# A planned scan-and-mixture kernel: one-chunk units at the start, ten late gate products on VectorE, six late copies on ScalarE, new ranks

## The chip, the cores and the metric

The kernel runs on one core of a Trainium2 chip. The metric is the device time of one execution in microseconds, the median over runs. A profile of a single execution gives a trace of every instruction on the engines: TensorE (PE, with its weight loads as PEld), VectorE (DVE), ScalarE (ACT), GpSimd (POOL), and SyncE (SP), which here only issues transfers.

## The reference

The input is a sequence `a`, `b` of 8 x 6400 rows of 128 numbers. A first-order recurrence runs along each sequence, and its output goes through a mixture of eight low-rank adapters, of which each row uses two.

```
h = a[:, t] * h + b[:, t];  out[:, t] = h          # scan, per batch, 6400 steps
x = out.reshape(51200, 128)
logits = x @ w_gate                                # 8 experts
topk = two largest;  w = softmax over the two
delta = sum over the two of w * ((x @ A[e]) @ B[e])    # rank 16
return x + delta
```

## The kernel before, in words

The 51,200 rows are cut into 100 chunks of 512 rows, each of four blocks of 128 rows. Rows arrive with time along the partitions, so each chunk is first turned.

The front of chunk c: `la`/`lb` load 256 KB of each input (two chunks in one transfer of 512 KB, except for the first `HEAD` chunks, which come singly); PE turns a into `pA` and b into `pB` (L562; for chunks loaded as a pair `P{c}` turns b of chunk c and a of chunk c+1 together, by half-height pieces); ACT copies `pA` to `a_st` (`ae`, L580); DVE runs the recurrence into `xT` (`sc`, L613), which continues from the last column of the chunk before.

A unit is a run of blocks, six before the tail, four in the last four units. `Z{u}` (L633) multiplies its blocks by A and the gate weights together into `pZ`, and ACT copies that to `zl` (`ze`, L639). Units are taken together in gate groups (four units, 24 blocks, six chunks, then smaller ones by `TAPER`). `gating` works out both largest logits and the weights for the whole group: maxima on DVE (`g1`, `g4`), the wide elementwise steps on POOL (`q2` to `q7`, L669 to L680) or, for the last six groups (`WIDE_DVE`), on DVE, a sigmoid on ACT (`w1`, L682), and the weights `g` on DVE (`g8`, L688).

The back of chunk c: the gate product `zw = zl * g` on POOL (`mu`, L707) or on DVE (`md`, L711); PE turns it (`T`, L720); the turned product is copied from PSUM to `zwT` by DVE (`te`, L729) or by ACT (L726); PE adds x itself (L734) and the product with B (L735) in `D`; ACT copies the sum to `outt` (`oe`, L744); SP stores two chunks at a time (`st`, L779), the last four singly.

The PSUM banks for T and D are two, used in turn (`place`): T of chunk c waits for `oe` of chunk c-2. For the last twelve chunks (`TAIL_CHUNKS`), once no more chunk has to be turned, the four banks of `pA` and `pB` join them. There are four `zw` buffers, six pair buffers for each input, 24 chunks of `xT` and 18 chunks of `outt`.

The order of the work is planned when the program is built. Every operation gets a rank: a base by its chunk, plus `TEMPLATE` by its kind, plus `NUDGE` by its name. `schedule` takes the operations engine by engine, the one that can begin first among those whose rank lies within `WINDOW` of the lowest, by its own assumed durations and rates (`LOAD_RATE`, `STORE_RATE`, `PAIR_RATE` and the like). The result is a fixed order on each of the five engines, and on SP the order of all transfers. At run time each engine goes through its list in order, and waits by semaphores only. Thus an operation that waits holds up whatever stands behind it on its engine.

These settings decide what the change touches: `HEAD` (chunks loaded singly), `LEAD` (sizes of the first gate groups, empty before), `TE_LAST` and `MU_DVE` (chunks counted from the end: 1 is chunk 99), `SPLIT` (stores that are cut into two transfers by partitions), `te_act`, `un`, and the list of units.

Of the kernel before, what the change touches and what calls it, by code (L numbers as in the profile page):

```python
# [10 lines left out]
PERIOD = 6  # L11
# [8 lines left out]
LOAD_RATE = 392e3  # L20
STORE_RATE = 408e3
# [86 lines left out]
START = (-999, "", 0)  # L108
FIRST = -9999
EARLY = -400  # L110
LEAD = []
TAPER = [2, 2, 1, 1, 1, 1]
WIDE_DVE = [1, 2, 3, 4, 5, 6]
TE_LAST = []
TAIL_UNITS = [4, 4, 4, 4]
TE_ACT = [1]
MU_DVE = [1, 2, 4, 6, 8]
TAIL_CHUNKS = 12
WARM0 = 12
WARM = 16  # L120
HALVES = 0.745
# [758 lines left out]
```

## Time and profile before

| what | value |
|---|---|
| median of 3 runs | 207.53 us (207.46 to 207.57) |
| the profiled execution's own time | 207.91 us |
| its span, first to last instruction | 205.9 us |
| its mean granted TensorE clock | 0.975 |
| moved by transfers | 79.26 MB, mean 385 GB/s |

Spans and starts in the rows below are counted from the first instruction of the profiled execution. In a row of a timeline stand the start, the duration, the engine, the line, the operation, the tiles (output, then inputs), the count, and in brackets how long the engine had been idle before and what released it. A row of the chain of waits has a start, a duration, an engine, a tile and a line. A row of the table by stretches has the busy time and the number of instructions of PE, PEld, DVE, ACT and POOL, then the granted TensorE clock, the DMA share and GB/s.

### The profile page before, as it was taken

The numbers are of one execution on the slowest core, as the hardware profiler recorded it, in microseconds if no ns is written. First come the engines' busy times: TensorE is split into PE (matmuls) and PEld (weight loads), VectorE is DVE, ScalarE is ACT, GpSimd is POOL, SyncE is SP. The second block draws the span as 40 slices with busy tenths as digits, with TensorE's granted clock in tenths as the row PEclk, the third lists the DMA queues.
The fourth block names the chain that finished last, engine by engine and source line by source line (L and its number), as shares of the span: only waits on it lengthen the run. The fifth ranks groups of instructions, "written<-read, shape, count | busy, mean of one in ns | idle before, by whom it ended". The sixth has DMA issues, their size and how long they took to land.

```text
span 205.9 us, 7539 instructions
## 1 busy us (share of the span) xinstructions
PE 184.7 (90%) x3152; PEld 160.9 (78%) x3152; DVE 177.7 (86%) x289; ACT 169.1 (82%) x306; POOL 144.6 (70%) x176
## 2 busy tenths in 40 slices
PE   7779589999998899899799999999999999879683
PEld 6557478887897789788689888988888888857572
DVE  0789688998998899798899999999997999989881
ACT  2356668999998999899799999999999998886372
POOL 1000328879898978878788988899989898687420
PEclk9999958999999999999999999999999999999789
DMA  6999999999999999999999999999999999997388
GB/s 191 368 392 415 405 409 406 405 409 405 411 417 406 414 403 417 409 403 416 408 409 400 409 395 408 415 410 411 409 412 410 410 409 404 405 352 289 132 299 300
DMA packets 30559, 79.26 MB, mean 385 GB/s; under 512 B 3774, under 2 KB 3902, under 8 KB 30526
## 3 DMA queue, kind: packets, MB, share of 16 engines
q1 hardware_dynamic: 29054, 78.39, 97.1%
q10 hardware_dynamic: 1472, 0.40, 0.8%
q8 instruction: 25, 0.41, 0.8%
q14 instruction: 8, 0.07, 0.1%
HBM read 52.56 MB, written 26.21 MB: 383 GB/s over the span
## 4 chain that ended last, share of the span: by engine, by line
PE 67%; DVE 12%; DMA 10%; POOL 3%; issue 3%; SPq 2%; ACT 1%; DVEq 0%; POOLq 0%
PE pA L562 14%; PE pB L562 12%; PE pZ L633 11%; PE pO L734 10%; PE pO L720 10%; PE pO L735 9%; DMA a_tm<-in_a_dram 7%; DVE xT L613 5%; DMA b_tm<-in_b_dram 3%; POOL zw L707 3%; SPq L541 2%; DVE zwT L729 2%; DVE zw L711 1%; ACT outt L744 1%; DVE g L688 1%
## 5 line engine op out<-in xcount | busy, mean ns | idle before, releaser
L613 DVE TENSOR_TENSOR_SCAN xT<-a_st,xT,pB 128x512 f16<-128x512 f32 x96 | 120.3, 1253 | 9.5 <-PE pA L562 5.6
L707 POOL TENSOR_TENSOR zw<-zl,g 128x512 f16<-128x512 f32 x95 | 100.4, 1069 | 24.7 <-PE pO L720 11.3
L562 PE MATMUL pB<-ident_f,b_tm 64*128 64x64 f32 (+1 forms) x768 | 71.4, 235 | 6.5 <-DMA a_tm<-in_a_dram 2.8
L580 ACT COPY a_st<-pA 128x512 f32<-128x512 f32 x100 | 60.5, 612 | 17.5 <-PE pA L562 16.0
L562 PE MATMUL pA<-ident_f,a_tm 64*128 64x64 f32 (+1 forms) x768 | 71.7, 235 | 2.0 <-DMA a_tm<-in_a_dram 1.0
L562 PEld LDWEIGHTS pB<-ident_f,b_tm 64*128 64x128 f32 (+1 forms) x768 | 57.9, 142 | 12.5 <-issue 3.7
L562 PEld LDWEIGHTS pA<-ident_f,a_tm 64*128 64x128 f32 (+1 forms) x768 | 57.9, 142 | 8.2 <-DMA a_tm<-in_a_dram 2.3
L639 ACT COPY zl<-pZ 128x816 f32<-128x816 f32 (+1 forms) x68 | 58.0, 853 | 2.3 <-PE pZ L633 1.6
L744 ACT COPY outt<-pO 128x512 f32<-128x512 f32 x92 | 52.7, 609 | 7.7 <-PE pO L735 7.3
L734 PE MATMUL pO<-ident_h,xT 128*128 128x128 f16 x368 | 50.1, 223 | 1.2 <-DVE zwT L729 1.0
L735 PE MATMUL pO<-cst_h,zwT 128*128 128x128 f16 x368 | 48.9, 220 | 0.8 <-issue 0.8
L734 PEld LDWEIGHTS pO<-ident_h,xT 128*128 128x128 f16 x368 | 40.5, 114 | 4.8 <-DVE zwT L729 2.1
L633 PE MATMUL pZ<-cst_h,xT 128*128 128x136 f16 x400 | 36.5, 228 | 1.5 <-DVE xT L613 0.6
L735 PEld LDWEIGHTS pO<-cst_h,zwT 128*128 128x128 f16 x368 | 36.9, 100 | 0.8 <-issue 0.8
L720 PE MATMUL pO<-ident_h,zw 128*128 128x128 f16 x368 | 33.2, 221 | 2.0 <-ACT outt L744 1.3
L729 DVE COPY zwT<-pO 128x512 f16<-128x512 f16 x77 | 30.2, 410 | 3.4 <-PE pO L720 3.1
L633 PEld LDWEIGHTS pZ<-cst_h,xT 128*128 128x128 f16 x400 | 27.1, 115 | 4.4 <-DVE xT L613 1.3
L720 PEld LDWEIGHTS pO<-ident_h,zw 128*128 128x128 f16 x368 | 22.3, 98 | 6.0 <-issue 1.9
L669 POOL TENSOR_TENSOR k<-zl,m 128x192 f32<-128x192 f32 x15 | 7.8, 519 | 22.9 <-DVE m L667 22.9
L671 POOL TENSOR_SCALAR L<-k 128x192 f32<-128x192 f32 x15 | 12.9, 860 | 1.3
L613 DVE TENSOR_TENSOR_SCAN xT<-a_st,pB 128x512 f16<-128x512 f32 (+1 forms) x8 | 7.5, 939 | 4.6 <-PE pB L562 4.3
L678 POOL TENSOR_TENSOR L<-k,m 128x192 f32<-128x192 f32 x15 | 7.9, 524 | 2.8 <-DVE m L676 2.7
(41 smaller groups left out, 106.1 us busy)
## 6 DMA issues: line engine op xcount, KB each, us to landing
a_tm<-in_a_dram SPq DMA_DIRECT2D x46, 512.0 KB, 10.7
b_tm<-in_b_dram SPq DMA_DIRECT2D x46, 512.0 KB, 10.6
out_dram<-outt SPq DMA_DIRECT2D x46, 512.0 KB, 10.8
a_tm<-in_a_dram SPq DMA_DIRECT2D x8, 256.0 KB, 5.8
b_tm<-in_b_dram SPq DMA_DIRECT2D x7, 256.0 KB, 6.0
out_dram<-outt SPq DMA_DIRECT2D x4, 256.0 KB, 2.7
out_dram<-outt SPq DMA_DIRECT2D x2, 480.0 KB
b_tm<-in_b_dram ACTq DMA_DIRECT2D x1, 256.0 KB, 3.6
```

Of the source, the lines that this page charges most:

```text
L562: last = eng["pe"].transpose(*args)
L580: lambda: eng["act"].copy(a_st[c % NA][:, :], pA[:, c % 2, :]), fr(c, "ae"))
L613: last = eng["dve"].tensor_tensor_scan(out=x[:, s0:s1], data0=a_st[c % NA][:, s0:s1], data1=pB[:, c % 2, s0:s1], initial=init, op0=ALU.mul ...
L633: last = eng["pe"].matmul(pZ[:, k // (n // 2), o : o + W], xblock(b0 + k), Awg_h)
L639: return eng["act"].copy(zl[:, zb : zb + n, :].rearrange("p (h k) w -> p h (k w)", h=2), pZ[:, :, 0 : n // 2 * W])
L671: lambda e: e.tensor_scalar(out=ll, in0=kk, scalar1=0.0, scalar2=-1.0e30, op0=ALU.is_ge, op1=ALU.mult), dve=not main)
L707: lambda: eng["pool"].tensor_tensor(out=wv, in0=zv, in1=gv, op=ALU.mult), ba(gi, c, "mu"))
L720: last = eng["pe"].transpose(ptile[:, k * 128 : k * 128 + 128], zw[w][:, k, :], ident_h[:, :])
L729: lambda: eng["dve"].tensor_copy(zwT[w][:, :], ptile[:, 0:C]), ba(gi, c, "te"))
L734: eng["pe"].matmul(dst, xblock(b0 + k), ident_h[:, :], start=True, stop=False)
L735: last = eng["pe"].matmul(dst, zwT[w][:, k * 128 : k * 128 + 128], B_h, start=False, stop=True)
L744: lambda: eng["act"].copy(outt[:, o0 : o0 + n, :].rearrange("p k w -> p (k w)"), bank),
```

## The change

The first 24 blocks are now six units of four blocks (one chunk each) and no longer four units of six; `LEAD` makes gate groups of one, two and three of them. Behind that the groups again cover six chunks each, on the same boundaries (chunks 6, 12, 18 and so on), and the last six groups cover the same chunks as before. Only the first four chunks are loaded singly; chunks 4 to 7 now come in pairs. The gate products of chunks 90 to 99 are all on DVE (before: 92, 94, 96, 98 and 99). The copies to `zwT` of chunks 90, 92, 94, 96, 98 and 99 go from DVE to ACT. The stores of chunks 56 and 78 were each cut into 120 and 8 partitions; now only that of chunk 56 is cut, into 125 and 3. All ranks and the windows are new, and three of the assumed rates.

```diff
-LOAD_RATE = 392e3
-STORE_RATE = 408e3
+LOAD_RATE = 387e3
+STORE_RATE = 413e3
...
-WINDOW = {'pe': 16.262, 'act': 17.153, 'dve': 47.02, 'pool': 47.064, 'sp': 57.831}
+WINDOW = {'pe': 32.272, 'act': 25.764, 'dve': 40.575, 'pool': 41.697, 'sp': 31.952}
...
-LEAD = []
+LEAD = [1, 2, 3]
...
-TE_LAST = []
+TE_LAST = [1, 2, 4, 6, 8, 10]
 TAIL_UNITS = [4, 4, 4, 4]
+HEAD_UNITS = [4, 4, 4, 4, 4, 4]
 TE_ACT = [1]
-MU_DVE = [1, 2, 4, 6, 8]
+MU_DVE = [1, 2, 3, 4, 5, 6, 7, 8, 9, 10]
...
-PAIR_RATE = 411e3
-HEAD = 8
+PAIR_RATE = 414.5e3
+HEAD = 4
...
-SPLIT = {56: [120, 8], 78: [120, 8]}
+SPLIT = {56: [125, 3]}
...
-    for n in [U] * ((NBLK - sum(TAIL_UNITS)) // U) + TAIL_UNITS:
+    for n in HEAD_UNITS + [U] * ((NBLK - sum(HEAD_UNITS) - sum(TAIL_UNITS)) // U) + TAIL_UNITS:
...
         def un(u, kind):
-            return (PERIOD * (u // GMAX), kind, u % GMAX)
+            v = u - len(HEAD_UNITS)
+            if v < 0:
+                return ((units[u][0] + units[u][1] - 1) // J - 1, kind, 0)
+            return (sum(HEAD_UNITS) // J + PERIOD * (v // GMAX), kind, v % GMAX)
```

What the planner makes of it, in the names used above (lists of the instruction order, no times in them):

```
PE, from chunk 96's turn on
before  P96 Z63 D77 T78 P97 T79 D78 Z64 P98 B99 Z65 T80 D79 D80 T81 T82 D81 ...
after   P96 T79 D78 D79 P97 T80 Z65 P98 T81 B99 D80 D81 Z66 T82 T83 D82 ...
D finished on PE ahead of P30, P60, P97:  before 10, 39, 78;  after 14, 39, 80
DVE, the end
before  sc97 g8(84-89) g2 g3 g5 ... te84 sc98 ... sc99 te86 ... te88 ... md94 ... md92 g8 te89 ... md96 ... md99 md98 te99 te98
after   g8(84-89) ... sc97 ... te80 te81 sc98 ... te82 sc99 te83 te84 ... te86 md90 ... te87 ... md91 ... te88 ... md92 ... te91 te89 md93 ...
        ... md96 ... te93 ... md97 ... md95 ... te97 ... md94 ... te95 ... md99 ... md98
POOL, the last gate products
before  ... mu89 mu90 mu91 mu95 mu93 mu97
after   ... mu87 mu88 mu89
SP, the first stores and the last loads
before  la30 lb30 st0 la32 lb32 la34 st2 lb34 ...     ... st58 la98 lb98 st60 st62 st64 ...
after   la30 lb30 la32 st6 lb32 la34 lb34 la36 st0 st8 st2 lb36 ...     ... st58 lb96 st60 la98 lb98 st62 st64 ...
```

More of the change, by code (lines that the diff above doesn't have):

```diff
@@ L121 @@
 HALVES = 0.745
-PAIR_RATE = 411e3
-HEAD = 8
+PAIR_RATE = 414.5e3
+HEAD = 4
 TAIL = 0
 STORE_TAIL = [1, 1, 1, 1]
-SPLIT = {56: [120, 8], 78: [120, 8]}
+SPLIT = {56: [125, 3]}
 TEMPLATE = {
-    "la": [-13.284, -13.376, -10.147],
-    "lb": [-12.856, -11.393, -13.112],
-    "A": [3.619, 4.619, -4.264, 6.619, 7.619, 8.619],
-    "B": [-2.245, 2.718, -8.407, 8.99, 6.061, 4.41],
-    "ae": [-1.493, 12.357, 10.831, 7.96, 5.931, 11.772],
-    "sc": [-2.149, -1.286, 6.521, -19.69, -9.638, -0.216],
-    "Z": [6.623, 2.916, -2.696, 9.959],
-    "ze": [6.413, 12.686, 18.636, 4.611],
-    "g1": [1.078],
-    "g2": [15.192],
-    "g3": [12.311],
-    "g4": [-7.624],
-    "g5": [43.586],
-    "g6": [18.91],
-    "w1": [27.261],
+    "la": [-13.694, -9.66, -7.958],
+    "lb": [-12.181, -8.232, -7.954],
+    "A": [0.032, 1.032, 2.032, 3.032, 98.725, 5.032],
+    "B": [-11.554, -16.992, -3.625, -1.674, -6.236, -9.416],
+    "ae": [-17.948, -9.336, -10.605, 9.499, -11.379, -1.476],
+    "sc": [-6.402, -11.561, 14.237, 14.579, 0.092, 8.857],
+    "Z": [15.334, 15.322, 3.164, 15.937],
+    "ze": [11.98, 9.742, 7.383, 9.214],
+    "g1": [12.595],
+    "g2": [-8.826],
+    "g3": [10.93],
+    "g4": [7.91],
+    "g5": [-34.789],
+    "g6": [-12.133],
+    "w1": [11.331],
     "w2": [27.183],
@@ L146 @@
     "p3": [35.473],
-    "mu": [22.377, 11.789, 38.051, -6.995, 25.901, 25.822],
-    "T": [17.564, 18.694, 15.643, 19.013, 20.568, 20.925],
-    "te": [11.47, 21.167, 12.791, -1.785, 1.996, 11.732],
-    "D": [13.525, 17.402, 15.169, 14.035, 19.652, 27.901],
-    "oe": [26.926, 32.894, 33.316, 36.556, 35.829, 26.06],
-    "st": [25.679, 26.621, 29.881],
-    "ta": [14.725, 30.746, 16.943, 18.052, 19.161, 20.27],
-    "md": [78.718, -0.018, -87.87, 12.1, 13.209, 14.318],
+    "mu": [30.508, 17.21, 42.13, 20.266, 33.206, 26.82],
+    "T": [8.415, 10.292, 10.959, 15.91, 26.88, 13.246],
+    "te": [3.828, 47.023, 6.141, 15.124, 6.753, 0.656],
+    "D": [15.16, 25.23, 10.659, 10.323, 8.93, 7.475],
+    "oe": [3.922, 6.15, 18.477, 24.064, 13.764, 12.977],
+    "st": [24.962, 26.75, 28.349],
+    "ta": [95.109, 11.785, 54.997, 19.327, 20.072, 20.817],
+    "md": [47.81, 33.679, 9.566, 18.407, 19.152, 19.897],
     "wu": [-0.198],
-    "ch": [26.813],
+    "ch": [-217.994],
     "mb": [0.0],
-    "q2": [17.668],
-    "q3": [-16.399],
-    "q5": [-0.842],
-    "q6": [-2.93],
-    "q7": [1.928],
+    "q2": [19.852],
+    "q3": [13.398],
+    "q5": [23.723],
+    "q6": [26.262],
+    "q7": [15.652],
     "q8": [35.473],
-    "g7": [47.426],
-    "g8": [9.111],
+    "g7": [3.758],
+    "g8": [-2.488],
 }
```

158 rows, old and new, of the table NUDGE are left out of this document.

## Prediction

> **What bounds the kernel now.** I read the throughput by slices first, then busy time by stretches, then SP's timeline, and last the chain of waits from 185 us on.
>
> ```profile
> span 205.9 us, 7539 instructions
> GB/s 191 368 392 415 405 409 406 405 409 405 411 417 406 414 403 417 409 403 416 408 409 400 409 395 408 415 410 411 409 412 410 410 409 404 405 352 289 132 299 300
> ```
> ```profile
> 0.00:10.00 10.00, 7.28 (x40) 6.11 (x41) 3.56 (x5) 3.25 (x5) 0.70 (x6) 1.00 0.84 276
> 20.00:30.00 10.00, 6.88 (x110) 5.75 (x110) 7.26 (x9) 6.30 (x11) 3.09 (x5) 0.80 1.02 407
> ...
> 170.00:175.00 5.00, 5.00 (x99) 4.48 (x100) 5.00 (x9) 4.37 (x9) 4.36 (x6) 1.00 1.04 403
> 175.00:180.00 5.00, 4.47 (x83) 4.03 (x83) 4.77 (x17) 4.24 (x8) 3.27 (x3) 1.00 1.06 406
> 180.00:185.00 5.00, 3.87 (x54) 2.90 (x51) 4.01 (x10) 3.94 (x9) 4.15 (x4) 1.00 0.96 357
> ```
>
> From the second slice to 180 us the transfers run at some 405 GB/s whatever the engines do (20 to 30 us: DVE 7.26 of 10 us, DMA share 1.02). There the bytes set the pace. Behind 180 us the rate falls to 289, 132, 299, 300: the stores wait for results.
>
> ```profile
> 161.92 0.47 SPq L541 DMA_DIRECT2D b_tm<-in_b_dram  x1
> 162.44 40.97 SPq L779 DMA_DIRECT2D out_dram<-outt  x23
> ```
> ```profile
> out_dram<-outt SPq DMA_DIRECT2D x17, 512.0 KB, 9.5
> out_dram<-outt SPq DMA_DIRECT2D x4, 256.0 KB, 2.7
> ...
> b_tm<-in_b_dram SPq DMA_DIRECT2D x1, 512.0 KB, 12.7
> out_dram<-outt SPq DMA_DIRECT2D x1, 480.0 KB
> out_dram<-outt SPq DMA_DIRECT2D x1, 32.0 KB
> ```
>
> The last load is issued at 161.92 and lands 12.7 us later, at 174.6. Behind it stand stores of 17 x 512 + 4 x 256 + 480 + 32 KB, 10.5 MB, at 405 GB/s 25.9 us: no order of the work could end the span before 200.5 while the loads land as they do. It ends at 205.9, so at most 5.4 us are to be had, and all of them behind 180 us. What holds the end there:
>
> ```profile
> 187.89 0.76 DVE zwT L729 x2
> ...
> 189.37 0.60 DVE zw L711
> 189.97 1.07 DVE k L680 x2
> 191.04 0.60 DVE zw L711
> 191.64 0.96 DVE g L688
> 192.60 0.34 DVE zwT L729
> ...
> 193.30 0.06 PE pO L734
> ...
> 193.41 0.11 PE pO L734
> ...
> 195.54 0.43 PE pO L720 x4
> ...
> 196.72 0.11 PE pO L735
> ...
> 197.05 0.24 PE pA L720 x4
> ...
> 198.83 0.23 DVE k L680 x2
> ...
> 199.39 0.20 DVE g L688 x2
> 199.59 1.24 DVE zw L711 x2
> ...
> 201.88 1.17 ACT outt L744 x2
> ```
> ```profile
> 189.90 2.65 POOL L707 TENSOR_TENSOR zw<-zl,g 128x512 f16<-128x512 f32 x2 [0.91 <-PE pA L720]
> ```
> ```profile
> 193.87 0.58 ACT L744 COPY outt<-pO 128x512 f32<-128x512 f32 x1 [2.98 <-PE pO L735]
> ```
>
> The chain is DVE's. Two tiny steps for k take 1.07 us while POOL has a gate product under way, and the same two 0.23 us at 198.83, when POOL has none; a small step for g takes 0.96 instead of 0.10 (0.20 for two). The copy at 192.60 stands behind them in DVE's order, so ACT goes without work for 2.98 us, and PE, with nothing to do, loses its clock:
>
> ```profile
> 190.00:192.00 2.00, 0.79 (x15) 0.62 (x13) 2.00 (x4) 0.89 (x3) 2.00 (x2) 1.00 0.74 279
> 192.00:193.00 1.00, 0.32 (x7) 0.15 (x4) 1.00 (x4) 0.00 (x0) 0.56 (x1) 1.00 0.18 68
> 193.00:194.00 1.00, 1.00 (x12) 1.00 (x13) 1.00 (x5) 0.13 (x1) 0.00 (x0) 0.64 0.03 10
> ...
> 195.00:196.00 1.00, 1.00 (x13) 1.00 (x11) 0.19 (x1) 0.49 (x2) 0.00 (x0) 0.50 0.64 240
> ```
>
> PE is busy 0.79 of 2 us and 0.32 of 1; then the granted clock is 0.64 and 0.50, and a matmul of the chain takes 0.11 us instead of 0.06, from 193.41 to 196.83.
>
> **The change part by part.** *The first six chunks.* Results of the first chunks come earlier: ahead of P30 fourteen D stand on PE instead of ten. Yet SP's order still has 32 chunks of loads ahead of the first store, and ahead of P60 the D are 39 in both. The transfers are full meanwhile, so this is worth nothing by itself. Its price, two more Z and two more zl copies, two more gate groups and smaller pieces in turning chunks 4 to 7, lies in stretches where DVE has 3.56 and 7.26 of 10 us and ACT 3.25 and 6.30. Without that cover it would be about a microsecond of ACT and DVE each, and the loads would still be ahead. The first pair loads being larger may lift the 368 GB/s of the second slice to 405, at most 5.15 x 37/405 = 0.5 us of the landing of everything behind; the other bound is no gain, and I take none, as the tail has slack from the loads. The cut stores (480 + 32 KB among those above) change no bytes: nothing.
>
> *A lead of one chunk.* Ahead of P97 stand 80 D instead of 78, ahead of P98 one chunk more. What a chunk takes in this stretch:
>
> ```profile
> 180.10 0.58 ACT L744 COPY outt<-pO 128x512 f32<-128x512 f32 x1 [0.38 <-PE pO L735]
> ...
> 189.19 0.59 ACT L744 COPY outt<-pO 128x512 f32<-128x512 f32 x1 [0.94 <-PE pO L735]
> ```
>
> Counted along ACT's order these are the copies of chunks 80 and 87: 9.09 us for seven, 1.30 each, as T waits for the bank of two chunks before. One chunk is worth -1.3 us at most and nothing if the last chunks are held by something else; I take -0.8, since the chain above is held by DVE.
>
> *Five gate products to DVE, six copies to ACT.* DVE gains 5 x 0.62 (half of 1.24) = 3.10 us and loses 6 x 0.38 (half of 0.76) = 2.28: +0.82. The scans of chunks 98 and 99 are moved ahead by two or three copies, which delays no copy more than the bank loop does.
>
> *POOL's late products gone.* POOL now ends with chunk 89. The collisions at 189.97 and 191.64 cost 1.07 - 0.23 = 0.84 and 0.96 - 0.10 = 0.86: -1.70 if they vanish, 0 if others take their place. I take -1.70: the products that collided (90 to 97) are the ones that leave.
>
> [...]
>
> *The clock.* With the hole at 190 to 193 gone PE should keep its clock. At full clock the 3.42 us from 193.41 would take 3.42 x 0.06/0.11 = 1.87: -1.55; the other bound is 0. I take half, -0.78: DVE hands PE the same chunks in a string of single products.
>
> *The last copies.* The copy behind the last product is now ACT's:
>
> ```profile
> L726 ACT COPY zwT<-pO 128x512 f16<-128x512 f16 x3 | 1.8, 597 | 0.0
> ```
>
> 0.60 instead of 0.38 us is +0.22; up to +0.6 if both last copies queue on ACT ahead of both outputs (1.17 us). The other four have cover in ACT's idle time (2.98 us in the one hole).
>
> The sum: -0.80 + 0.82 - 1.70 - 0.78 + 0.22 = -2.24 us, a span of 203.7. The profiled execution took 207.91, so it would take 205.67; the median shown is 0.38 lower, so the forecast is 205.3.
>
> **The rivals.** *The collisions only move.* md90 stands on DVE right behind te86, which is due when POOL still has products 87, 88 and 89 to do. If each of the three holds up DVE by 0.85, that is +2.55 instead of the 1.70 that went: +0.85 in place of -1.70, and the sum is +0.31: 207.8. For it: the chance overlap cost 0.8 to 0.9 each time above. Against: products 87 to 89 are due within 3.2 us, and md90 needs weights that are due no sooner.
>
> *PE falls to half its clock (slower).* Place: the last twelve chunks. If DVE's products, queued ahead of copies (md90 before te87, md91 before te88), leave PE under half busy for 3 us, as at 190 to 193, and PE then doesn't recover between products, a chunk's 12 matmuls take 12 x 0.11 = 1.32 us, twelve chunks 15.8 us. Before, they took from 189.78 (end of chunk 87's copy) to 203.05, 13.3 us. That is +2.5, less 0.8 of lead: +1.7, 209.2. It decides from the point where DVE spends more than about 1.3 us a chunk. Against: products, half the copies and the small steps come to about 1 us a chunk. [...]
>
> *SP waits for a store.* Store 6 stands behind the first load of chunk 32 and waits for chunk 7's output, with all loads behind it. If it waits longer than what is under way (a load lands 12.7 us after its issue late in the run), the transfers run dry; 1.5 us of that would give 209.0, and it would show as a slice under 390 GB/s before 180 us. Against: the first outputs come earlier, not later.
>
> **How the numbers follow.** Forecast 0.56; collisions that move 0.16 (207.8: mostly no change); half clock 0.20; SP 0.08. Within 0.2% (0.4 us, about what a measurement of this kernel can tell) counts as no change. Faster: 0.56 and 0.04 of the first rival; same: 0.08 of it; slower: 0.20 + 0.08 and the last 0.04 of it, 0.32. The likeliest one's own range: all gains at their bounds, -1.30 + 0.82 - 1.70 - 1.55 + 0.22 = -3.5, and 0.5 from the loads, give 203.5, and 203.3 with ACT's copies free as well; with neither lead nor clock it is -0.66, 206.9. The whole range reaches up to 208.7: the first rival is inside, and of the case with every gain at 0 and the copies at +0.6 (+1.42, 208.95) nearly all.
>
> **What would show it.** Right: last load landing within 0.5 us of 174.6; no DVE step of 32 elements over 0.5 us behind 187; no idle time of ACT near 3 us; PE at clock 1.00 from 190 to 200; copies of chunk 87 about a microsecond earlier. Wrong: slices under 390 GB/s before 180 us (SP), DVE products of over 0.9 us (collisions), a granted clock near 0.5 for more than 4 us behind 187.

## The result and the profile after

| | before | after |
|---|---|---|
| median, 16 runs each beside one another | 207.38 us (206.29 to 207.96) | 208.92 us (207.66 to 210.86) |
| profiled execution, its span | 207.91 us, 205.9 us | 209.14 us, 207.3 us |
| mean granted TensorE clock of it | 0.975 | 0.98 |

After over before is 1.0062 (95%: 1.0040 to 1.0083): the change makes the kernel 0.6% slower, where 205.3 us was forecast and 208.7 was the top of the range. The two slowest runs of after (210.78 and 210.86) belong to a slower state and are left out of this ratio, as such runs are of every ratio below; the median of the other 14 is 208.59.

The throughput by slices of the kernel after, from its page (a slice is a fortieth of the span, 5.18 us):

```profile
span 207.3 us, 7603 instructions
GB/s 189 382 410 405 410 405 410 405 380 343 358 411 406 409 419 409 408 409 409 409 410 412 411 405 410 412 413 413 407 414 413 383 408 403 400 286 275 217 366 245
```

Two things differ from the row of before. Slices 9 to 11 (41 to 57 us) have 380, 343 and 358 instead of 409, 405 and 411: there the transfers ran dry, that is, too few were under way to keep the queue full. And almost nothing shows near 170 us: one slice has 383 (161 to 166 us), and from 166 on the rate is 408, 403 and 400, about as before; yet that is where the engines stand still. Busy time by stretches, kernel after (PE, PEld, DVE, ACT, POOL with counts, granted clock, DMA share, GB/s):

```profile
40.00:50.00 10.00, 9.93 (x194) 8.75 (x195) 9.59 (x15) 9.06 (x17) 8.38 (x11) 1.00 1.00 371
50.00:60.00 10.00, 9.83 (x187) 8.62 (x185) 9.59 (x15) 9.77 (x18) 9.02 (x12) 1.00 1.02 371
170.00:175.00 5.00, 3.51 (x46) 3.08 (x47) 1.77 (x3) 2.57 (x5) 1.32 (x2) 0.68 1.02 403
...
190.00:195.00 5.00, 4.63 (x69) 3.89 (x69) 4.93 (x22) 4.24 (x10) 0.17 (x1) 1.00 0.57 211
```

From 170 to 175 us DVE works 1.77 of 5 us (before: 5.00) at an unchanged 403 GB/s. Behind 190 us the tail looks as the prediction had it: PE at clock 1.00 and 4.63 of 5 us busy, POOL all but done (0.17 us).

What SP did in the two places (kernel after, SP's timeline; start, duration):

```profile
39.03 0.33 SPq L549 DMA_DIRECT2D a_tm<-in_a_dram  x1
45.19 0.40 SPq L787 DMA_DIRECT2D out_dram<-outt  x1
45.63 0.47 SPq L549 DMA_DIRECT2D b_tm<-in_b_dram  x1
...
153.68 1.83 SPq L787 DMA_DIRECT2D out_dram<-outt  x2
155.55 1.35 SPq L549 DMA_DIRECT2D a_tm<-in_a_dram  x1
...
166.97 1.24 SPq L549 DMA_DIRECT2D b_tm<-in_b_dram  x1
168.25 36.74 SPq L787 DMA_DIRECT2D out_dram<-outt  x21
```

From 39.36 (39.03 + 0.33) SP issues nothing until 45.19: the entry there is the store of chunks 6 and 7, and chunk 7's copy to `outt` ends at 45.2. The load behind it goes out at 45.63; the same load went out at 40.17 before. At 153.68 the two pieces of chunk 56's store go out, 125 and 3 partitions, and right behind them the `a` load of chunk 94. The times from issue to landing of that load and of the last one (kernel after, transfers issued in 155.5 to 155.6 and in 166.9 to 167.0):

```profile
a_tm<-in_a_dram SPq DMA_DIRECT2D x1, 512.0 KB, 15.9
...
b_tm<-in_b_dram SPq DMA_DIRECT2D x1, 512.0 KB, 13.7
```

The first lands at 155.55 + 15.89 = 171.44, the last at 166.97 + 13.7 = 180.6, six microseconds behind the 174.6 of before. The chain of waits of the kernel after shows who waited for it, and its ACT and DVE timelines what stood meanwhile (in brackets the idle time and its releaser):

```profile
155.55 15.89 DMA a_tm<-in_a_dram
171.49 0.27 PE pB L570
```
```profile
167.62 0.59 ACT L752 COPY outt<-pO 128x512 f32<-128x512 f32 x1
170.27 0.58 ACT L752 COPY outt<-pO 128x512 f32<-128x512 f32 x1 [2.06 <-DMA out_dram<-outt]
```
```profile
172.49 1.28 DVE L621 TENSOR_TENSOR_SCAN xT<-a_st,xT,pB 128x512 f16<-128x512 f32 x1 [3.29 <-PE pA L570]
```

ACT's wait at 168 to 170 is for the cut store itself: the copy is chunk 74's, which needs the place of chunk 56 in `outt`, 18 chunks back. DVE's scan waits 3.29 us for the late load.

The account of the span: before, 10.49 MB of stores stood behind the last load, 25.9 us, and the span ended 205.9 - 174.6 - 25.9 = 5.4 us behind what these bytes take. After, one pair store fewer stands there (21 issues, 9.96 MB, 24.6 us at 405 GB/s), and 207.3 - 180.6 - 24.6 = 2.1 us are left. So the tail did get 3.3 us better, and what lies ahead of it lost 6.0 - 1.3 = 4.7. The difference is the 1.4 us of the two spans.

### The profile page after: what moved, and what is told of

Read it like the earlier page. It is cut to its first block, busy times and chain, and to the rows that moved or that the text cites. A ratio compares the mean times of both kernels' runs of the same rounds, so it can differ in the third digit from the quotient of the medians.

```text
span 207.3 us, 7603 instructions
## 1 busy us (share of the span) xinstructions
PE 182.9 (88%) x3184; PEld 158.2 (76%) x3184; DVE 175.5 (85%) x294; ACT 173.6 (84%) x316; POOL 141.0 (68%) x181
## 4 chain that ended last, share of the span: by engine, by line
PE 40%; DMA 14%; DVE 8%; ACT 4%; POOL 3%; issue 3%; DVEq 0%
PE pA L570 8%; DMA a_tm<-in_a_dram 8%; PE pB L570 7%; PE pO L742 7%; DMA b_tm<-in_b_dram 7%; PE pO L728 7%; PE pZ L641 6%; PE pO L743 5%; DVE zw L719 2%; ACT outt L752 2%; DVE zwT L737 2%; DVE xT L621 2%; POOL zw L715 2%; ACT zl L647 1%; ACT zwT L734 1%
## 5 line engine op out<-in xcount | busy, mean ns | idle before, releaser
L621 DVE TENSOR_TENSOR_SCAN xT<-a_st,xT,pB 128x512 f16<-128x512 f32 x96 | 120.2, 1252 | 13.7 <-PE pA L570 7.2
L715 POOL TENSOR_TENSOR zw<-zl,g 128x512 f16<-128x512 f32 x90 | 94.4, 1060 | 25.8 <-PE pO L728 14.0
L728 PE MATMUL pO<-ident_h,zw 128*128 128x128 f16 x368 | 34.5, 222 | 3.5 <-POOL zw L715 2.0
L677 POOL TENSOR_TENSOR k<-zl,m 128x192 f32<-128x192 f32 (+3 forms) x17 | 8.3, 490 | 13.0 <-DVE m L675 12.8
L679 POOL TENSOR_SCALAR L<-k 128x192 f32<-128x192 f32 (+3 forms) x17 | 13.3, 784 | 1.5
L686 POOL TENSOR_TENSOR L<-k,m 128x192 f32<-128x192 f32 (+3 forms) x17 | 8.2, 479 | 6.6 <-DVE m L684 6.6
```

The lines of the kernel that those rows point to most:

```text
L621: last = eng["dve"].tensor_tensor_scan(out=x[:, s0:s1], data0=a_st[c % NA][:, s0:s1], data1=pB[:, c % 2, s0:s1], initial=init, op0=ALU.mul ...
L679: lambda e: e.tensor_scalar(out=ll, in0=kk, scalar1=0.0, scalar2=-1.0e30, op0=ALU.is_ge, op1=ALU.mult), dve=not main)
L715: lambda: eng["pool"].tensor_tensor(out=wv, in0=zv, in1=gv, op=ALU.mult), ba(gi, c, "mu"))
L728: last = eng["pe"].transpose(ptile[:, k * 128 : k * 128 + 128], zw[w][:, k, :], ident_h[:, :])
```

## The experiments

All ratios are against the kernel before, run beside each on the same chip. The first question was whether the cut store or the wait of SP made the loads late.

**1. The cut alone, on both kernels.** Four kernels: after with the old cuts, after without cuts, before with the new cut, before without cuts.

```diff
-SPLIT = {56: [125, 3]}
+SPLIT = {56: [120, 8], 78: [120, 8]}      (a_split_old)
+SPLIT = {}                                (a_split_none)
```
```diff
-SPLIT = {56: [120, 8], 78: [120, 8]}
+SPLIT = {56: [125, 3]}                    (b_split_new)
+SPLIT = {}                                (b_split_none)
```

> The changed kernel with only the cut stores as before (56 and 78 in 120 + 8 partitions). Theory A (the end follows the last load's landing, which came 6.0 us later for three reasons: transfers that ran dry at 45 to 57 us behind store 6, one store more ahead, and the cut 125 + 3, which makes the 16 parts of every later transfer finish 9.4 instead of 5.7 us apart): no jump behind store 56, last load lands near 178 instead of 180.6, time near 207.4 (-1.5). Theory B (DVE's ten products and ACT's copies set the end whatever the loads do): landing may move, the time stays at 208.9 within 0.3.

> The changed kernel with no store cut. Theory A: the parts stay about 5.7 us apart, last load near 178, time near 207.4, the same as with the old cuts, since only the uneven 125 does harm. If the old cuts are themselves a help, this one is slower than the old cuts by 0.5 us or more. Theory B: 208.9 within 0.3.

> The kernel before with only the new cut (store 56 in 125 + 3, store 78 whole). Theory A: the parts of the transfers behind store 56 spread by 3 to 4 us more, the last load lands near 177.5 instead of 174.6, time 208.5 to 209.5 (+1 to +2). Theory B, or a cut that costs nothing, as predicted: 207.4 within 0.3.

> The kernel before with no store cut. Theory A: the old cuts neither skew nor mend much, 207.4 within 0.5; if they mend a drift among the 16 parts, spread grows beyond 5.9 us and the time is 208 or more.

| kernel | median us | ratio to before (95%) | last load lands |
|---|---|---|---|
| a_split_old | 205.78 | 0.9945 (0.9916 to 0.9975) | 177.0 |
| a_split_none | 206.15 | 0.9935 (0.9910 to 0.9961) | 178.2 |
| b_split_new | 208.97 | 1.0103 (1.0074 to 1.0133) | 177.5 |
| b_split_none | 207.34 | 1.0007 (0.9984 to 1.0030) | 174.4 |

The cut into 125 and 3 costs 1.0103 - 1.0007, 1.0% or 2.0 us (1.6 by the medians), in the old order, and 1.0062 - 0.9935, 1.3% or 2.6 us, in the new; the cut into 120 and 8 costs nothing that shows. One line turned a slightly faster kernel into a slightly slower one.

How can a cut that moves the same bytes do this? Each load has 16 completion records in the traces: it is carried in 16 parts that finish separately. By the time of issue, the time between the first and the last of the 16, in the two profiled executions:

```
after    issued 151.8: 5.71    155.6: 9.38    156.9: 7.95    164.1: 7.72 us
before   issued 151.0: 4.79    156.9: 5.07    161.9: 5.25 us
```

Right behind the cut store the spread jumps from 5.71 to 9.38 us and then stays near 8. The theory from it: a transfer is dealt to the largest number of parts, at most 16, that divides its partitions. 125 goes to 5 parts, each with 500 / 5 = 100 KB instead of 32; at 410 / 16 = 25.6 GB/s a part, these five are 70 KB or 2.7 us late for everything behind. 120 goes to 15.

The records of the stores agree with these counts. A whole store leaves 16. That of 125 and 3 leaves ten in the kernel after: one behind each of its two issues (154.99 and 155.69 us) and eight from 164.47 to 170.20, as five and three make. That of 120 and 8 in its place leaves 25 in the kernel before: again one behind each issue (155.01 and 157.00) and 23, as fifteen and eight make.

The completions of the loads bear out the five. The records don't name the parts, but they can be matched by time: of the 16 completions of the load issued at 155.55, eleven come 1.2 to 1.3 us behind one of the load issued at 151.78, the last ahead of the cut, as if they had nothing of the store to carry (32 KB at 25.6 GB/s take 1.3 us), and five come 5.2 to 5.5 us behind theirs (100 and 32 KB: 5.3 us). Four of these five had been ahead and land within the others, at 165.90 to 167.10 us. The fifth had been among the last; it lands at 171.44, 3.9 us behind the fifteenth completion and 1.24 behind the last record of the store, and the load is there only with this last part: PE begins on it at 171.49. When it is, 2.5 MB issued behind it have already moved, against 1.4 MB for the load ahead of the cut. That is why the rate in GB/s shows next to nothing.

By the theory the one part of a store of 127 partitions, which no number from 2 to 16 divides, would carry all its 508 KB. That makes a sharp test.

**2. One part.** The kernel before, its cut set to 127 and 1:

```diff
-SPLIT = {56: [120, 8], 78: [120, 8]}
+SPLIT = {56: [127, 1]}
```

> The kernel before with store 56 cut into 127 + 1 partitions and store 78 whole: it measures how a cut store is dealt among the 16 parts. Theory D (a transfer is dealt to the largest number of parts, 16 or fewer, that divides its partitions: 125 goes to five, with 100 KB each instead of 32, which at 25.6 GB/s is 2.7 us; 120 goes to 15): 127 goes to one part, 508 KB instead of 32 is 18.6 us: the completions of the next transfers spread by some 23 us, the last load lands near 193, time 218 to 226. Theory E (dealt in equal runs of bytes, the skew of 125 has another cause): spread within 1 us of before, 207 to 208.

One run: 223.22 us, span 221.2. SP's timeline and busy time by stretches of it:

```profile
153.88 19.36 SPq L779 DMA_DIRECT2D out_dram<-outt  x2
173.29 0.39 SPq L541 DMA_DIRECT2D b_tm<-in_b_dram  x1
```
```profile
150.00:160.00 10.00, 9.69 (x178) 8.33 (x177) 8.60 (x14) 9.09 (x18) 9.17 (x11) 1.00 1.03 410
160.00:170.00 10.00, 9.75 (x186) 8.55 (x182) 9.66 (x15) 9.68 (x18) 9.18 (x11) 1.00 0.33 130
170.00:180.00 10.00, 0.00 (x0) 0.00 (x0) 0.66 (x3) 0.11 (x1) 1.51 (x3) 0.68 0.57 179
```
```profile
166.00:168.00 2.00, 2.00 (x40) 1.73 (x39) 1.84 (x2) 2.00 (x5) 1.92 (x3) 1.00 0.07 26
172.00:174.00 2.00, 0.00 (x0) 0.00 (x0) 0.00 (x0) 0.00 (x0) 0.00 (x0) 0.90 0.07 27
```

508 KB on one part are 520 KB (of 1000 bytes) / 25.6 GB/s = 20.3 us of that part; SP is held for 19.36 us in issuing the two pieces, the other parts run out of issued work, and from 166 us on the rate is 26 to 34 GB/s at a DMA share of 0.07 to 0.11 (one part of 16 is 0.06): one part at work, at its 25.6 GB/s and hardly above. PE has no matmul for ten microseconds. The cost is 223.22 - 207.51 = 15.7 us. Two of the signs expected did not come: the last load lands at 189.2 and not near 193, and the loads behind spread by 6.6 us at most and not by 23, as SP issues none before 173.29. For the sizes tried here, dealing by the largest divisor is shown: by the 16 records of 128, the eight of 125 and 3, the 23 of 120 and 8, and the one part at work with 127. That the parts serve their transfers in order is read from the spread that stays, 7.65 to 7.95 us for the five loads behind the first one in the kernel after.

**3. The wait of SP, and three other parts, without the cut.** From here on `SPLIT = {}` unless told. The order of SP is changed behind the planner, by moving one store; the same few lines serve for every move below, with other names:

```diff
+        for e, name, behind in [('sp', 'st6', 'la36')]:
+            line = P.order[e]
+            op = line.pop([o.name for o in line].index(name))
+            line.insert([o.name for o in line].index(behind) + 1, op)
```

c_st6 moves the store of chunks 6 and 7 behind the `a` load of chunk 36, ahead of store 0. c_st60 moves the store of chunks 60 and 61 behind the last load instead. c_prod_pool puts the products 90, 91, 93, 97, 95 back on POOL, c_copy_dve the six copies back on DVE, each behind the step named with it:

```diff
+BACK_POOL = [90, 91, 93, 97, 95]
-lambda: eng["dve"].tensor_tensor(out=wv, in0=zv, in1=gv, op=ALU.mult)
+lambda: eng["pool" if c in BACK_POOL else "dve"].tensor_tensor(out=wv, in0=zv, in1=gv, op=ALU.mult)
```
```diff
+BACK_DVE = [(90, 'te87'), (92, 'te89'), (96, 'te93'), (94, 'te95'), (99, 'md98'), (98, 'te99')]
```

> The changed kernel with no store cut, and with the store of chunks 6 and 7 moved in SP's order from behind the first load of chunk 32 to behind the first load of chunk 36. Theory A (every delay of the loads reaches the end): the loads of chunks 32 to 36 are issued from 40 us on instead of 45.6, the transfers stay above 395 GB/s at 40 to 60 us (349 and 364 with no cut), the last load lands near 176 instead of 178.2, time 205.0 (-1.1). Theory C (with the cut gone, the last 12 chunks are held by DVE, and loads two us earlier only wait longer): landing moves, time within 0.4 of 206.15.

> The changed kernel with no store cut, and with the store of chunks 60 and 61 behind the last load, as in the kernel before. Theory A: the last load lands 1.3 us earlier, near 177.0, time 205.5 (-0.6). Theory C: time within 0.4 of 206.15.

> The changed kernel with no store cut, and with the gate products of chunks 90, 91, 93, 95 and 97 back on POOL (last in POOL's order), every other order kept. If the gain of the tail comes from POOL's products leaving (predicted -1.70 of collisions and -0.78 of clock against +0.82 net of work, with the copies staying on ACT), the time rises to about 207 to 208, single steps of DVE behind 187 us take 0.8 us and more again, and the granted clock falls below 0.9 behind 190. If POOL's products did no harm, it falls by up to 1 us, as DVE has 3.1 us less to do.

> The changed kernel with no store cut, and with the copies of chunks 90, 92, 94, 96, 98 and 99 back on DVE, every other order kept. As the sum has it, DVE gets 6 x 0.38 = 2.3 us more in the last 15 us, where it is busy all the time: time 207 to 208. If ACT's slower copies are what holds the end, it falls by 0.2 us or more.

| kernel | median us (lowest to highest) | ratio to before (95%) |
|---|---|---|
| c_st6 | 204.05 (203.70 to 204.40) | 0.9830 (0.9814 to 0.9846) |
| c_st60 | 208.34 (206.30 to 209.98) | 1.0011 (0.9979 to 1.0043) |
| c_prod_pool | 206.39 (204.68 to 206.94) | 0.9926 (0.9896 to 0.9956) |
| c_copy_dve | 205.28 (204.79 to 205.33) | 0.9882 (0.9865 to 0.9898) |

The store of chunks 6 and 7 costs 0.9935 - 0.9830, 1.05% or 2.2 us. Stretches of a_split_none:

```profile
40.00:50.00 10.00, 10.00 (x196) 8.79 (x195) 9.50 (x14) 9.33 (x17) 8.24 (x11) 1.00 0.94 349
50.00:60.00 10.00, 9.83 (x188) 8.62 (x186) 9.59 (x15) 9.69 (x19) 9.02 (x12) 1.00 1.02 364
```

and SP's timeline and stretches of c_st6:

```profile
40.97 0.33 SPq L549 DMA_DIRECT2D b_tm<-in_b_dram  x1
...
45.69 3.61 SPq L787 DMA_DIRECT2D out_dram<-outt  x4
```
```profile
40.00:50.00 10.00, 9.93 (x192) 8.67 (x191) 9.59 (x15) 9.12 (x17) 8.38 (x11) 1.00 1.03 408
50.00:60.00 10.00, 9.82 (x187) 8.66 (x186) 9.58 (x15) 9.63 (x18) 9.01 (x12) 1.00 1.03 405
```

With the store moved, the load goes out at 40.97 and the rate is 408 and 405 GB/s; each engine's work in either ten microseconds is the same to about 0.2 us. In the kernel after 20 us at 371 against 406.5 are 0.71 MB, 1.75 us, and no later stage gives them back. The last load lands at 175.4, with SP's wait at 178.2 (a_split_none), with wait and cut at 180.6 (after): of the 6.0 us against before, 2.8 are the wait's, 2.4 the cut's and 0.8 the rest's. The runs also scatter less: 0.7 us between the lowest and the highest of five instead of 1.8 among the nine of a_split_none.

c_st60 fell as an idea. The last load does land earlier, at 175.4 instead of 178.2, but the kernel is not faster: 0.8% or 1.6 us slower than a_split_none by the ratios. Its ACT waits from 170 to 185 us:

```profile
ACT outt L752 <- DMA out_dram<-outt: 2.2, 1, 2.2
```

The copy that waits is chunk 78's, 18 chunks behind 60: the moved store lands at 176.9 and ACT, with every output behind it, stands until then. The profiled execution is the fastest of the twelve (206.30 us, as fast as that of a_split_none, 206.46): it shows how the 2.8 us of earlier landing are lost again, and not what the slower runs lose beyond that. This store's place ahead of the last loads is not a defect but what the ring of 18 chunks asks for.

c_prod_pool equals a_split_none. c_copy_dve seemed 0.5% faster than it (four runs), but in its profiled execution the stretches from 40 to 60 us are milder, so that the two can't be compared for the copies alone:

```profile
40.00:50.00 10.00, 10.00 (x193) 8.91 (x190) 9.73 (x15) 9.90 (x19) 8.24 (x11) 1.00 1.01 383
50.00:60.00 10.00, 9.84 (x186) 8.59 (x184) 9.59 (x15) 9.78 (x18) 9.01 (x12) 1.00 1.03 384
```

So both edits had to be tried where SP does not wait.

**4. Products and copies on the base of c_st6.** d_prod_pool, d_copy_dve and d_both undo the one, the other and both, with the lines shown.

> No store cut, store 6 behind the first load of chunk 36 (204.05, and steady), and the five gate products 90, 91, 93, 95, 97 back on POOL. Predicted for the products: -1.66 us with the collisions and the net of work (+0.82 - 1.70 - 0.78), so 205.5 or more here. If, as with store 6 in its place, the engine of the products doesn't matter: 204.05 within 0.3.

> No store cut, store 6 behind the first load of chunk 36, and the six copies back on DVE. If DVE's work in the last 15 us sets the end, 2.3 us more of it give 205.5 to 206.3. If ACT's slower copies cost as much as they spare: 204.05 within 0.3.

> No store cut, store 6 behind the first load of chunk 36, and both the products and the copies on the engines of the kernel before; the order is otherwise the new one. If the two edits carry the gain of the last 25 us, the time goes back to 206 or more (207.4 before). If the new order carries it (scans 98 and 99 ahead of chunks 82 and 83, a lead of one to two chunks), it stays under 205.

They took 203.89, 204.35 and 204.00 us: 0.9828 (0.9798 to 0.9857), 0.9851 (0.9821 to 0.9881) and 0.9830 (0.9800 to 0.9860), against 0.9830 of c_st6. By the medians neither move is worth more than 0.3 us, in either direction; the intervals allow some 0.6 us more. Stretches of d_both, and DVE and POOL in it:

```profile
185.00:190.00 5.00, 4.59 (x71) 3.96 (x71) 4.97 (x23) 3.25 (x9) 2.18 (x3) 1.00 0.85 323
190.00:195.00 5.00, 3.43 (x52) 2.75 (x50) 4.93 (x18) 2.80 (x7) 2.08 (x2) 1.00 0.93 342
```
```profile
191.81 0.99 DVE L684 TENSOR_TENSOR L<-L,k 128x32 f32<-128x32 f32 x1
```
```profile
190.68 2.08 POOL L721 TENSOR_TENSOR zw<-zl,g 128x512 f16<-128x512 f32 x2 [1.07 <-DVE k L679]
```

With products on POOL again, the collision is back (0.99 us for a step of 32 elements under POOL's products from 190.68 on), and the clock is 1.00 all the same and the time unchanged. So the collision is there in the two kernels with products on POOL at 191 us (1.07 us for two steps before, 0.99 for one here) and not in the kernel after, where POOL has none from 190.17 on and no such step takes over 0.19. It costs nothing that shows here; the lost clock of before went with the new order, not with these two edits.

**5. Where the gain comes from, and the other stores.** f_scan_late puts the scans of chunks 98 and 99 in c_st6 back behind te84 and just ahead of te86, near where the old order had them; f_before_scan makes the opposite move alone in the kernel before, with the two copies `ae` that they need. f_st60 is c_st6 with store 60 behind the last load. f_swap, on after without the cut, moves three stores: 0 behind la32, 6 behind la36, 60 behind lb98.

```diff
+('dve', 'sc98', 'te84'), ('dve', 'sc99', 'g3_19')                            (f_scan_late)
+('act', 'ae98', 'oe79'), ('act', 'ae99', 'ae98'),
+('dve', 'sc98', 'te81'), ('dve', 'sc99', 'te82')                             (f_before_scan)
+('sp', 'st60', 'lb98')                                                       (f_st60)
+('sp', 'st0', 'la32'), ('sp', 'st6', 'la36'), ('sp', 'st60', 'lb98')         (f_swap)
```

> No store cut, store 6 behind the first load of chunk 36 (204.05), and the scans of chunks 98 and 99 back where the kernel before has them in DVE's order, behind the copy of chunk 84 and ahead of that of chunk 86. If the early scans carry the gain of the last 25 us: 205.3 or more, and ACT's hole and a granted clock under 0.9 come back behind 187. If it is the lead of the whole back (outputs of chunks 80 to 88 2.3 us earlier): 204.05 within 0.4.

> No store cut, store 6 behind the first load of chunk 36, and store 60 behind the last load as in the kernel before. The last load lands 1.3 us earlier, near 174.1. If the end still follows the landing: 203.2 or less. If not: 204.05 within 0.3.

> The kernel before, with the scans of chunks 98 and 99 (and their copies on ACT) as early as in the changed one: behind the copies of chunks 81 and 82. If the early scans alone fill the hole at 190 to 193 us, 206.3 or less (-1.2); if the lead counts, 207.4 within 0.4, the scans only delaying copies 82 to 84.

> No store cut; store 0, whose output is ready at 28 us, in the place of store 6 in SP's order, store 6 behind the first load of chunk 36, store 60 behind the last load. No wait is left between 38 and 48 us, so DMA stays above 400 GB/s; a candidate for the best: 203.2 to 204.0. Slower than 204.4 would say that a store ahead of the loads of chunks 32 to 36 costs more than the wait.

| kernel | median us | ratio to before (95%) |
|---|---|---|
| f_scan_late | 205.11 | 0.9920 (0.9892 to 0.9947) |
| f_st60 | 207.03 | 0.9969 (0.9937 to 1.0001) |
| f_before_scan | 207.57 | 1.0024 (0.9996 to 1.0052) |
| f_swap | 206.53 | 0.9955 (0.9922 to 0.9987) |

f_st60 and f_swap lose 2.5 to 3.0 us to c_st6, and the wait that c_st60 showed is back (ACT stands 2.0 us for a store in f_swap); that it is the whole of the loss is not shown. In f_swap the rate from 38 to 48 us is 406 GB/s, so SP's wait there is gone, but f_st60, which lacks only the move of store 0, is as slow by the intervals. The scans' place is worth 1.1 us by the medians and 1.9 by the ratios in the new order and nothing that shows in the old; why not there was not followed further. Stretches of f_scan_late:

```profile
180.00:185.00 5.00, 2.37 (x37) 1.91 (x34) 4.91 (x12) 3.08 (x6) 2.98 (x4) 1.00 1.00 377
185.00:190.00 5.00, 4.38 (x66) 3.79 (x67) 4.19 (x19) 3.71 (x9) 0.39 (x1) 1.00 0.68 259
```

With the two scans there, DVE is busy 4.91 of 5 us and PE has work for 2.37, at a clock that stays at 1.00, other than expected; output 87 begins at 189.0 instead of 186.9, and the rate behind it is 259 GB/s where c_st6 has 327.

**6. The price of the cut without the wait, and stores still earlier.** g_st6_cut is the kernel after, cut included, with store 6 moved as in c_st6. g_early is c_st6 with store 58 behind lb94 and store 60 behind la96, each ahead of its old place.

```diff
+('sp', 'st6', 'la36')                                                        (g_st6_cut)
+('sp', 'st6', 'la36'), ('sp', 'st58', 'lb94'), ('sp', 'st60', 'la96')        (g_early)
```

> The changed kernel as it is, cut of store 56 included, with only store 6 moved behind the first load of chunk 36. Against 204.05 with no cut and the same move, this gives the price of the cut alone. Theory A: chunk 74's output waits some 2 us for store 56 and the loads behind it land 2.5 us later, 206.5 to 207. If the cut hurts only together with the dry transfers: 204.5 or less.

> No store cut, store 6 behind the first load of chunk 36, stores 58 and 60 each one transfer earlier. With store 60 one load later, the output copy of chunk 78 waited 2 us for its 18-chunk-old buffer and all came 3 us later. If these waits still bind (copies 76 and 78 begin within 0.5 us of stores 58 and 60 landing), 203.3 to 203.9; if the loads then land too late, 204.3 or more.

g_st6_cut took 206.99 us, 0.9977 (0.9957 to 0.9998): the cut alone costs 206.99 - 204.05 = 2.9 us here (0.9977 - 0.9830 or 3.0 us by the ratios), the store's wait alone 1.0062 - 0.9977, 0.85% or 1.8 us. The same place in ACT's timeline with the cut, and in c_st6 without it:

```profile
165.20 0.59 ACT L752 COPY outt<-pO 128x512 f32<-128x512 f32 x1
167.97 0.58 ACT L752 COPY outt<-pO 128x512 f32<-128x512 f32 x1 [2.18 <-DMA out_dram<-outt]
```
```profile
165.52 1.07 ACT L752 COPY outt<-pO 128x512 f32<-128x512 f32 x2
```

Where the copies of two chunks follow one another without the cut, 2.18 us lie between them with it. g_early took 204.36 us, 0.9837 (0.9810 to 0.9865): no gain, so the stores ahead of the last loads are not late.

## Why the prediction was wrong

**The step that failed** is one sentence, "The cut stores [...] change no bytes: nothing". The bytes are the same, the number of parts that carry them is not. It cost 2.6 us of the result (1.6 to 3.0 over the three pairs of kernels with and without it), and the prediction had no range for it. The rows of before could not have shown it, as 120 and 8 partitions cost nothing there (1.0007 without them). The completion records give the parts: eight for 125 and 3 against 23 for 120 and 8. Either loss alone would have left the time within the range, 206.15 us without the cut and 206.99 without the wait below; it took both to pass 208.7.

**The rival "SP waits for a store"** came true beside it, with the mechanism, the place and the sign that it gave: slices of 380, 343 and 358 before 180 us. It asked 1.5 us of dry transfers, and 1.75 to 2.2 were paid. What was wrong was its chance of 0.08 and the argument against it, that the first outputs come earlier. They do, chunk 7's copy at 44.5 to 45.2 instead of 51.5 to 52.0, some 7 us. But the store moved up further, from 52.06 to directly behind a load issued at 39.03. The comparison to make was between the two moves, not between output and old output. The six chunks 6 to 11 are one gate group in the new order, and chunk 7 waits for the weights of all six. That the rival's 209.0 us stands so near to the measured 208.92 is chance: it put 1.5 us on the time of before, with no gain from the order, while the wait alone leaves 206.15, and the rest is the cut's.

**The lead of a chunk (-0.80)** had the right sign and was too small. In c_st6 outputs 80, 84 and 88 end at 178.4, 183.3 and 188.6, before at 180.7, 185.3 and 190.9: 2.0 to 2.3 us earlier, although the last load lands 0.8 us later. Chunk 87's copy begins at 186.9 instead of 189.2, which the prediction named as its sign (about a microsecond). In the kernel after it begins at 193.1, behind the late loads. The prediction counted D in PE's order and missed that the whole front of work is ahead: outputs 12, 24 and 60 end 5.6, 4.0 and 4.1 us earlier in c_st6. How much of this the first six chunks give and how much the new ranks was not tried; "worth nothing by itself" for the head stays open.

**Products and copies (+0.82), the late copies (+0.22), collisions (-1.70), the clock (-0.78).** As tied to the two edits, all four are wrong: undone together they change nothing that shows. The signs that they named do come: in the kernel after the longest single step of 32 elements behind 187 us takes 0.19 us, the longest idle time of ACT there is 0.74 us, and PE's clock is 1.00 from 190 to 200. But d_both has the clock with the old engines, and a collision of 0.99 us that nobody pays for. Even the products that d_prod_pool takes off DVE, five of 0.68 us, bring 0.16 us. That the span of c_st6 is already within 1.9 us of its floor (below) fits this, but what holds these last 1.9 us was not tried apart. In c_st6 from output 80 on 24.1 us pass to the end of the span, before 25.8: that is the 1.7 us that the tail itself gained.

**The sum** of the terms was -2.24 us, and what the change gives without the two losses is -3.5 by the ratio (-3.4 by the medians, 204.05 against 207.45). With some 2.6 and 2.0 us lost at the two stores this makes +1.1, where +1.3 was measured by the ratio and +1.5 by the medians. As both losses were measured as differences between these same kernels, the sum can't fail by much and proves nothing more.

**The other rivals.** Half clock did not come: it was to decide where PE is under half busy for 3 us, and in f_scan_late PE works 2.37 of 5 us at clock 1.00, so the place of the decision was wrong as well. Collisions that only move did not come either: the ten products on DVE behind 187 us take 0.68 us each on average, as the groups of the kernel after show (line, shapes, count, busy time, mean ns, idle time before):

```profile
L719 DVE TENSOR_TENSOR zw<-zl,g 128x512 f16<-128x512 f32 x10 | 6.8, 682 | 0.0
```

**What bounds the kernel** held: the span of after ends 2.1 us behind the floor that the last load and the stores behind it set, and c_st6, with that load landing at 175.4, ends at 201.9, 1.9 us behind its own (175.4 + 24.6 = 200.0). The prediction left out what makes this a floor. Counted over all parts less is left when the last load lands, 9.3 MB before and 7.5 after by the rows of GB/s, as most parts are ahead by then. The part that lands last, though, has by an estimate from the 16 records of each store its whole sixteenth of the stores still to move, 655 KB before, 25.9 us at 405 / 16 = 25.3 GB/s, and b_split_127 shows a part alone hardly faster (26 to 27). The sign "last load within 0.5 us of 174.6" was the one that gave the failure away.

The kernel without the cut and with store 6 moved (c_st6, or d_prod_pool and d_both, which are equal to it) beats both: 204.05 us, 1.7% under before.

## What to carry to other kernels

Before cutting a transfer, look at how many partitions each piece has: here 120 cost nothing, 125 some 2 to 3 us and 127 some 16 (one run), and the transfers behind paid: the load behind the 125 was complete 9.38 us after its first part instead of 5.71, and PE began on it only with its last part. A rate of 400 to 408 GB/s, as here, says next to nothing of this; the time from issue to landing and the spread of completions do. Where a new order moves a store up among loads, compare the moment at which the queue reaches it with the moment at which its output is ready, and where it moves a store back, count who needs the place that it frees.

## What the runs showed of the hardware

- A store of 125 partitions put five of the 16 parts some 4 us behind the other eleven; the load behind it was complete 9.38 us after its first part instead of 5.71, and the lag was still there nine microseconds later (7.72). A store of 127 left one part at work: SP was held for 19.36 us, and the rate was 26 to 34 GB/s from 166 to 174 us.
- With nothing of the kind the parts still drift apart: in the run before, the 16 completions of one load lie at most 2.1 us apart for loads issued in the first 70 us, and 4.8 to 5.3 us apart for those issued from 151 us on.
- PE kept its clock at 1.00 through 5 us in which it was busy for 2.37 (f_scan_late), while it fell to 0.64 in the kernel before right behind 3 us with 0.79 of 2 and 0.32 of 1 us busy.
